# Top-k attention and GELU MLP: two of the four top-k rounds on a joined row, and a new order of ScalarE's steps

## The chip, the cores and the metric

The kernel runs on one core of a Trainium2 chip. A time is device microseconds of one execution. Beside the timed runs, one execution was taken by the hardware profiler; its rows are what is quoted below. The engines are PE (TensorE: matmuls; PEld is its weight load), DVE (VectorE), ACT (ScalarE), POOL (GpSimd) and SP (SyncE, here the DMA queue).

## The reference

Attention over 8 batches, 8 heads, 576 positions and 64 dimensions, in which each row keeps its 32 largest scores; then an MLP with exact GELU on the 4608 tokens.

```python
scores = scale * np.matmul(q, k.transpose(0, 1, 3, 2))            # 8 x 8 x 576 x 576
kth = np.partition(scores, -32, axis=-1)[..., -32:-31]
scores = np.where(scores >= kth, scores, -1e9)
attn = np.exp(scores - scores.max(-1, keepdims=True))
attn = attn / (attn.sum(-1, keepdims=True) + 1e-9)
x = np.matmul(attn, v)                                            # to (4608, 512)
h = x @ w_in                                                      # (4608, 2048)
out = (0.5 * h * (1 + erf(h / sqrt(2)))) @ w_out                  # (4608, 512)
```

## The kernel before, in words

**Items.** The work on attention is cut into 144 items, 18 for each batch. An item is a block of 128 query rows for two heads (e = 0, 1), so its scores are a tile `s` of 128 partitions by 2 x 576 values. The last 64 rows of each batch are put together from two pairs of heads. Where two batches meet, one has these items at its end and the next at its start.

**The order is written out by hand.** A loop over steps n = 0 to 147 issues, for several items at different stages, the instructions of each engine in the order in which that engine runs them; each engine works strictly through its own list and waits on semaphores. In step n:

- PE makes the scores of item n + 2 (`scores`, L370, and the last keys at L333 or L347), the product with v of item n - 3 (`attend`, L629), and the transposes of item n - 2 (`transposes`, L539 for the last keys and L565 for the others). Pieces of the MLP stand between these: L687 is the first layer into `h_ps`, L829 and L831 the second. Up to START (n = 10) there is no MLP work to put there, and `keep_busy` (L1015) issues a fixed number of filler matmuls instead.
- ACT copies the scores out of PSUM (L341, L378), runs the softmax of item n - 1 (`softmax`), copies the transposes (`pt`, L549, L572, L581), the attention output (`xT`, L634) and q and k (`qm`, `kt`, L286), and makes the GELUs (L703).
- DVE finds the 32nd largest score of item n in each row (`top_k`), with the reciprocal of item n - 1's sum put in near the end (`inverse`, L495).
- POOL makes the smaller list of item n + 1 (`smaller`, L431), adds 1e-9 to the sum of item n - 1 (`add_small`, `den`, L501), makes `neg` and `bias` of item n out of `kth` (`threshold`, L488, L489), multiplies item n - 1 by its reciprocal (`normalise`, L520), begins the lists of item n + 2 (`sum_up`, L423), and then takes small additions of the MLP (L724 to L727, L852 and L881 to L896).

**Top-k on pairs.** In 134 items (all but items 18 to 27, `SINGLE`) the 576 values of a row are split into two halves of 288, a and b. DVE makes the larger of each pair (`larger`, L406), POOL the smaller as a + b - larger in integer arithmetic. The two lists lie behind each other in a tile `lists` of 128 x 2 lists x 2 heads x 288. MAX8 (L463) finds the 8 largest of a list, MATCH_REPLACE8 (L466) overwrites them, and that is a round, for both heads. Before, the larger list has four rounds (32 values, the last without replacing) and the smaller list two (16 values, the second without replacing). The 17th to 32nd of the larger list and the 16 of the smaller one in reverse are then compared pairwise (L478), and the least of the results (L479) is `kth`, in a tile of its own. For items 0 and 1 the rest of the larger list goes to a tile `rest_g`. In the ten items that are not paired the same rounds run four times over all 576 values, and `kth` is the last value of `top`. `top` has one buffer.

**Softmax.** For each head, L508 applies a steep Prelu that throws out all that is below `kth`, in place, and L509 reads the result and makes the exponential and its sum. In steps up to START both heads follow each other with little between (the copy of `xT` in some steps).

**Weights.** For each of steps 1 to 10 and 13 to 18, at the end of the step before, a block of the MLP's weights is widened from its loaded form (`weights_size`): L205 and L206 on ACT, where L206 reads what L205 wrote, then L212, which works on another part and needs neither. In some of the later steps L208 on DVE takes the place of L212. POOL adds the two results (L227).

Of the kernel before, what the change touches and what calls it, by code (L numbers as in the profile page):

```python
# [8 lines left out]
TOPK = 32  # L9
LOWEST = -3.4028234e38  # L10
STEEP = 2.0**100
# [3 lines left out]
def kernel(  # L15
# [42 lines left out]
    scale = 1.0 / float(D) ** 0.5  # L58
# [4 lines left out]
    work = ctx.enter_context(tc.tile_pool(name="work", bufs=2))  # L63
# [90 lines left out]
    low = const.tile([P, 1], f32, name="low")  # L154
# [39 lines left out]
    def parts(u):  # L194

        t, dst = words[u], weights_of(u)[3].bitcast(i32)
        return t[:, :, 0::2], t.bitcast(mybir.dt.int16)[:, :, 2::4], t[:, :, 1::2], dst

    def weights_size(u):


        if u not in words:
            return
        w, first, below, d = parts(u)
        nc.scalar.activation(below, first, func=AF.Prelu, bias=high, scale=2.0**-40, alpha=2.0**40)  # L205
        nc.scalar.activation(d, below, func=AF.Prelu, bias=low, scale=2.0**59, alpha=2.0**-40)  # L206
        if on_dve(u):
            nc.vector.tensor_scalar(  # L208
                w.bitcast(i32), w.bitcast(u32), 2.0**-13, None, op0=ALU.mult
            )  # L210
        else:
            nc.scalar.activation(w.bitcast(i32), w.bitcast(u32), func=AF.Copy, scale=2.0**-13)  # L212

    def on_dve(u):

        return SLOT_OF[u] in ON_DVE

    def waits(u):

        return u == ORDER[-1]  # L220
# [25 lines left out]
    N = len(items)  # L246
# [60 lines left out]
    S_of, stat_of = {}, {}  # L307

    def row(i, e):
        return S_of[i][:, e * S : (e + 1) * S]  # L310
# [81 lines left out]
    lists_of = {}  # L392
    HS = S // 2

    def paired(i):

        return PAIRED <= i < N and i not in SINGLE

    def halves_of(i):
        s = S_of[i].rearrange("p (e h n) -> p e h n", e=2, h=2)  # L400
        return s[:, :, 0], s[:, :, 1]

    def larger(i):

        if paired(i):
            nc.vector.tensor_tensor(lists_of[i][:, 0], *halves_of(i), op=ALU.max)  # L406

    def first_lists():

        lists_of[0] = t = work.tile([P, 2, 2, HS], f32, tag="lists", name="lists")  # L410
        a, b = halves_of(0)
        for e in range(2):
            nc.vector.tensor_tensor(t[:, 0, e], a[:, e], b[:, e], op=ALU.max)
        top, both = t[:, 0].bitcast(i32), t[:, 1].bitcast(i32)
        nc.gpsimd.tensor_tensor(both, a.bitcast(i32), top, op=ALU.subtract)
        nc.gpsimd.tensor_tensor(both, both, b.bitcast(i32), op=ALU.add)

    def sum_up(i):

        if paired(i):  # L420
            lists_of[i] = t = work.tile([P, 2, 2, HS], f32, tag="lists", name="lists")
            a, b = halves_of(i)
            nc.gpsimd.tensor_tensor(  # L423
                t[:, 1].bitcast(i32), a.bitcast(i32), b.bitcast(i32), op=ALU.add
            )

    def smaller(i):

        if paired(i):
            both, top = lists_of[i][:, 1].bitcast(i32), lists_of[i][:, 0].bitcast(i32)  # L430
            nc.gpsimd.tensor_tensor(both, both, top, op=ALU.subtract)  # L431

    def top_k(i, last):


        stat_of[i] = st = {
            "first": work.tile([P, 2, 8], f32, tag="first", name="first"),
            "kth": work.tile([P, 2], f32, tag="kth", name="kth"),
            "neg": work.tile([P, 2], f32, tag="neg", name="neg"),
            "bias": work.tile([P, 2], f32, tag="bias", name="bias"),  # L440
            "den": work.tile([P, 2], f32, tag="den", name="den"),
            "rden": work.tile([P, 2], f32, tag="rden", name="rden"),
        }
        half_k = TOPK // 2
        top = work.tile([P, 2, TOPK - 8], f32, tag="top", bufs=1, name="top")
        low = work.tile([P, 2, half_k], f32, tag="low", bufs=1, name="low")
        into = [st["first"]] + [top[:, :, 8 * r : 8 * r + 8] for r in range(TOPK // 8 - 1)]
        if paired(i):
            t = lists_of.pop(i)
            rest = t[:, 0]  # L450
            if i < 2:
                rest = work.tile([P, 2, 512], f32, tag="g", bufs=2, name="rest_g")[:, :, 0:HS]
            rounds = [(t[:, 0] if r == 0 else rest, rest, x) for r, x in enumerate(into)]
            rounds += [(t[:, 1], t[:, 1], low[:, :, 8 * r : 8 * r + 8]) for r in range(half_k // 8)]
            ends = (len(into) - 1, len(rounds) - 1)
        else:
            s = S_of[i].rearrange("p (e n) -> p e n", e=2)
            t = work.tile([P, 2, S], f32, tag="lists", name="rest")
            rounds = [(s if r == 0 else t, t, x) for r, x in enumerate(into)]
            ends = (len(rounds) - 1,)  # L460
        for r, (src, dst, x) in enumerate(rounds):
            for e in range(2):
                nc.vector.max(x[:, e], src[:, e])  # L463
            if r not in ends:
                for e in range(2):
                    nc.vector.match_replace(dst[:, e], x[:, e], src[:, e], LOWEST)  # L466
# [7 lines left out]
        backwards = bass.AP(  # L474
            tensor=low.tensor, offset=low.offset + half_k - 1,
            ap=[list(low.ap[0]), [half_k, 2], [-1, half_k]],
        )
        nc.vector.tensor_tensor(upper, upper, backwards, op=ALU.max)  # L478
        nc.vector.tensor_reduce(  # L479
            st["kth"].rearrange("p (e x) -> p e x", x=1), upper, mybir.AxisListType.X, ALU.min  # L480
        )

    def threshold(i):

# [12 lines left out]
    def add_small(i):  # L497
# [2 lines left out]
        st = stat_of[i]  # L500
        nc.gpsimd.tensor_scalar(st["den"], st["den"], 1e-9, None, op0=ALU.add)  # L501

    def softmax(i, e):

        if i < 0 or i >= N:
            return
        st, s = stat_of[i], row(i, e)
        nc.scalar.activation(s, s, func=AF.Prelu, bias=st["neg"][:, e : e + 1], scale=1.0, alpha=STEEP)  # L508
        nc.scalar.activation(  # L509
            s, s, func=AF.Exp, bias=st["bias"][:, e : e + 1], scale=1.0,  # L510
            accum_out=st["den"][:, e : e + 1],
        )
# [84 lines left out]
    def copy_x():  # L597
        while copies:
            copies.pop()()
# [445 lines left out]
    for pair in range(2, n_pairs):  # L1045
        b, p = divmod(pair, NP)
# [9 lines left out]
    for n in range(ahead):  # L1056
# [7 lines left out]
        if n > 0:  # L1064
            larger(n + 1)
# [29 lines left out]
        if not few[0] and n > START:  # L1095
            softmax(n - 1, 0)
# [33 lines left out]
        if n > 0:  # L1130
            smaller(n + 1)
# [74 lines left out]
```

## Time and profile before

| | before |
|---|---|
| median of 3 runs | 1535.11 us (1534.01 to 1535.32) |
| the profiled execution's own time | 1534.11 us |
| its span, from the first to the last instruction | 1532.3 us |
| mean granted clock of TensorE | 0.998 |
| HBM read and written | 45.08 MB, 9.44 MB |

A row of the list of groups reads: line, engine, operation, output <- inputs, shapes, number of instructions, then busy time, mean duration in ns of one, and idle time of the engine just before it with what ended most of it. A row of the order of time reads: start in us from the span's start, duration in us, engine, line, operation, output <- inputs, shape, number merged into the row, and in brackets the idle time before it and what ended that. A row of a stretch of time reads: the stretch and its length, then for PE, PEld, DVE, ACT and POOL the busy time and the number of instructions, the granted clock, the busy share of the DMA engines and GB/s. A row of the waits reads: who waited for whom, us in total, how many times, and the longest.

### The profile page before, as it was taken

The page shows a single profiled execution, that of the slowest core. Times are in us where ns is not written, and L with a number is a line of the kernel's source. Part 1 is how long each engine was busy: PE and PEld are TensorE (multiplying, and loading weights), DVE is VectorE, ACT ScalarE, POOL GpSimd, SP SyncE. Part 2 cuts the span into 40 slices and gives each one's busy share as a digit, 9 for nine tenths or more (in the row PEclk, how much of TensorE's full clock was granted, in tenths as well). Part 3 has the DMA queues.
Part 4 walks back from the last instruction along what each step waited for, and adds up shares of the span by engine and source line. Part 5 has one row for each costly group of instructions (what it writes and reads, how often), then busy time and mean ns, then how long its engine had stood idle before and what let it go on. Part 6 is the DMA issues. An engine that isn't in the chain of part 4 may idle for free.

```text
span 1532.3 us, 28123 instructions
## 1 busy us (share of the span) xinstructions
PE 1513.8 (99%) x9240; PEld 1194.1 (78%) x9240; DVE 1336.5 (87%) x4610; ACT 1160.1 (76%) x2038; POOL 1144.5 (75%) x1291
## 2 busy tenths in 40 slices
PE   7999999999999999999999999999999999999999
PEld 5786677887777777888877778788787777788887
DVE  7999999999989988899989998989998998888801
ACT  6999977777877687877777777787777868787730
POOL 6897667767787878777787877776788786877742
PEclk9999999999999999999999999999999999999999
DMA  6434310012101110012201111012110111000000
GB/s 169 135 108 114 87 46 1 21 35 37 24 19 28 38 40 15 1 30 47 40 15 20 27 32 46 1 25 36 32 24 22 24 30 32 15 1 15 8 14 14
DMA packets 195026, 56.35 MB, mean 37 GB/s; under 512 B 185888, under 2 KB 186432, under 8 KB 194880
## 3 DMA queue, kind: packets, MB, share of 16 engines
q1 hardware_dynamic: 193616, 54.14, 15.2%
q8 instruction: 72, 1.18, 0.3%
q14 instruction: 74, 0.61, 0.1%
q10 hardware_dynamic: 1200, 0.39, 0.1%
q0 software_dynamic: 64, 0.03, 0.0%
HBM read 45.08 MB, written 9.44 MB: 36 GB/s over the span
## 4 chain that ended last, share of the span: by engine, by line
PE 75%; POOL 11%; DVE 5%; ACT 1%; issue 1%; DVEq 0%; POOLq 0%
PE h_ps L687 27%; PE y_ps L831 15%; PE o L629 8%; PE tp L565 6%; PE s_ps L370 6%; POOL s L520 3%; PE seven L829 2%; PE y_ps L775 2%; PE y_ps L793 2%; PE y_ps L796 2%; POOL lists L423 1%; POOL lists L431 1%; DVE lists L466 1%; PE tp_t L333 1%; PE o L640 1%; DVE top L463 1%
## 5 line engine op out<-in xcount | busy, mean ns | idle before, releaser
L687 PE MATMUL h_ps<-xT,w_in_sb 128*128 128x256 f32 (+1 forms) x2560 | 544.2, 361 | 0.2
L687 PEld LDWEIGHTS h_ps<-xT,w_in_sb 128*128 128x128 f32 x2560 | 434.0, 191 | 71.1 <-issue 25.2
L463 DVE MAX8 top<-lists 128x8 f32<-128x288 f32 x792 | 321.3, 447 | 0.0
L520 POOL TENSOR_TENSOR s<-s,rden 128x1152 f32<-128x1152 f32 x144 | 302.7, 2102 | 0.3 <-DVE rden L495 0.3
L509 ACT ACTIVATE s<-s,bias 128x576 f32<-128x576 f32 x288 | 223.4, 776 | 11.9
L466 DVE MATCH_REPLACE8 lists<-top,lists 128x288 f32<-128x288 f32 x528 | 229.9, 443 | 0.0
L508 ACT ACTIVATE s<-s,neg 128x576 f32<-128x576 f32 x288 | 225.7, 784 | 4.0 <-POOL neg L488 3.9
L581 ACT COPY pt<-tp 128x1024 f32<-128x1024 f32 x133 | 135.2, 1017 | 112.1 <-PE tp L565 112.1
L463 DVE MAX8 low<-lists 128x8 f32<-128x288 f32 x536 | 216.4, 446 | 0.0
L431 POOL TENSOR_TENSOR lists<-lists 128x576 int32<-128x576 int32 x133 | 187.6, 1410 | 4.0
L501 POOL TENSOR_SCALAR den<-den 128x2 f32<-128x2 f32 x144 | 31.4, 218 | 213.0 <-ACT s L509 208.8
L423 POOL TENSOR_TENSOR lists<-s 128x576 int32<-128x576 int32 x133 | 187.0, 1406 | 0.0
L488 POOL TENSOR_SCALAR neg<-kth 128x2 f32<-128x2 f32 x134 | 86.9, 649 | 99.2 <-DVE kth L479 98.1
L629 PEld LDWEIGHTS o<-pt,raw_v 128*64 128x64 f32 x1280 | 87.3, 137 | 86.5 <-issue 45.4
L629 PE MATMUL o<-pt,raw_v 128*64 128x256 f32 x1280 | 153.8, 385 | 0.7 <-ACT pt L572 0.4
L565 PE MATMUL tp<-ident,s 128*128 128x128 f32 x1152 | 149.6, 273 | 0.0
L565 PEld LDWEIGHTS tp<-ident,s 128*128 128x128 f32 x1152 | 134.7, 141 | 14.7 <-issue 1.9
L831 PE MATMUL y_ps<-w_out_sb,sum 128*128 128x256 f32 x472 | 140.4, 379 | 0.0
L370 PE MATMUL s_ps<-kt,qm 64*128 64x512 f32 x512 | 131.1, 626 | 0.8 <-ACT s L376 0.8
L378 ACT ACTIVATE s<-s_ps 128x1024 f32<-128x1024 f32 x127 | 124.0, 1024 | 8.9 <-PE s_ps L370 8.8
L495 DVE RECIPROCAL rden<-den 128x2 f32<-128x2 f32 x144 | 23.2, 161 | 115.3 <-POOL den L501 114.1
L466 DVE MATCH_REPLACE8 lists<-low,lists 128x288 f32<-128x288 f32 x268 | 116.7, 443 | 0.0
(164 smaller groups left out, 2770.9 us busy)
## 6 DMA issues: line engine op xcount, KB each, us to landing
raw_v<-in_v_dram SPq DMA_DIRECT2D x64, 128.0 KB, 2.4
out_dram<-y SPq DMA_DIRECT2D x30, 256.0 KB, 2.1
raw_q<-in_q_dram SPq DMA_DIRECT2D x112, 64.0 KB, 2.0
raw_k<-in_k_dram SPq DMA_DIRECT2D x112, 64.0 KB, 2.0
w_out_sb<-in_moe_w_in_dram SPq DMA_DIRECT2D x14, 511.8 KB, 4.7
w_out_sb<-in_moe_w_out_dram SPq DMA_DIRECT2D x10, 511.8 KB, 4.3
w_sum<-in_moe_w_out_dram SPq DMA_DIRECT2D x6, 511.8 KB, 4.7
raw_q<-in_q_dram SPq DMA_DIRECT2D x112, 8.0 KB, 1.8
```

The source lines that it names most:

```text
L370: nc.tensor.matmul(s_ps[:, e], lhsT=q_t[rows, :], rhs=kt[rows, 0:SM], start=True, stop=True)
L423: nc.gpsimd.tensor_tensor(t[:, 1].bitcast(i32), a.bitcast(i32), b.bitcast(i32), op=ALU.add)
L431: nc.gpsimd.tensor_tensor(both, both, top, op=ALU.subtract)
L463: nc.vector.max(x[:, e], src[:, e])
L466: nc.vector.match_replace(dst[:, e], x[:, e], src[:, e], LOWEST)
L508: nc.scalar.activation(s, s, func=AF.Prelu, bias=st["neg"][:, e : e + 1], scale=1.0, alpha=STEEP)
L509: nc.scalar.activation(s, s, func=AF.Exp, bias=st["bias"][:, e : e + 1], scale=1.0, accum_out=st["den"][:, e : e + 1],)
L520: nc.gpsimd.tensor_tensor(s, s, wide, op=ALU.mult)
L565: nc.tensor.transpose(tp[:, j * P : (j + 1) * P], s[:, first + j * P : first + (j + 1) * P], ident)
L629: nc.tensor.matmul(o[e * D : (e + 1) * D, 0:n], lhsT=vt[:, j, e, :], rhs=pt[:, e * NM + j if j < NM else 2 * NM, :], start=(j == 0), stop= ...
L687: nc.tensor.matmul(h_tile(u)[:, i, :], lhsT=w_in_sb[:, ko, f * P : (f + 1) * P], rhs=xT[:, ko, c0 : c0 + n], start=(ko == 0), stop=(ko == ...
L831: nc.tensor.matmul(acc[names][:, k], lhsT=lhsT, rhs=rhs, start=(j == 0 and k == 0), stop=(j == FT // 2 - 1 and k == 1),)
```

## The change

- In paired items the two lists now lie side by side for each head (128 x 2 heads x 2 lists x 288), so that both together are one row of 576 values. Two rounds run on the larger list, with replacing; then two rounds run on the joined row, which holds what is left of the larger list and the smaller list, the last without replacing. The pairwise comparison and the minimum are gone, and `kth` is the last value of `top` in all items.
- For items 0 and 1 the joined row is a tile `into`, which uses the buffer of `pt`, in place of `rest_g`.
- The instruction that follows L205 in `weights_size` is now the one on the other part, and the one that reads L205's result comes third.
- In steps up to START the Prelus of both heads are issued before the first exponential.

Line numbers of the changed file differ by a few: L463 becomes L465, L466 L468, L423 L431, L431 L439, L488 and L489 L479 and L480, L501 L492, L520 L522, L495 L486, L508 L499, L509 L511, L539 L541, L687 L689.

```diff
         nc.scalar.activation(below, first, func=AF.Prelu, bias=high, scale=2.0**-40, alpha=2.0**40)
-        nc.scalar.activation(d, below, func=AF.Prelu, bias=low, scale=2.0**59, alpha=2.0**-40)
         if on_dve(u):
...
             nc.scalar.activation(w.bitcast(i32), w.bitcast(u32), func=AF.Copy, scale=2.0**-13)
+        nc.scalar.activation(d, below, func=AF.Prelu, bias=low, scale=2.0**59, alpha=2.0**-40)
...
     def larger(i):
         if paired(i):
-            nc.vector.tensor_tensor(lists_of[i][:, 0], *halves_of(i), op=ALU.max)
+            nc.vector.tensor_tensor(lists_of[i][:, :, 0], *halves_of(i), op=ALU.max)
+
+    def into_of(i):
+        if i < 2 and i not in into_lists:
+            into_lists[i] = work.tile([P, 2, 2, HS], f32, tag="pt", bufs=1, name="into")
+        return into_lists.get(i, lists_of[i])
...
     def sum_up(i):
...
-                t[:, 1].bitcast(i32), a.bitcast(i32), b.bitcast(i32), op=ALU.add
+                t[:, :, 1].bitcast(i32), a.bitcast(i32), b.bitcast(i32), op=ALU.add
...
     def smaller(i):
         if paired(i):
-            both, top = lists_of[i][:, 1].bitcast(i32), lists_of[i][:, 0].bitcast(i32)
-            nc.gpsimd.tensor_tensor(both, both, top, op=ALU.subtract)
+            both, top = lists_of[i][:, :, 1].bitcast(i32), lists_of[i][:, :, 0].bitcast(i32)
+            nc.gpsimd.tensor_tensor(into_of(i)[:, :, 1].bitcast(i32), both, top, op=ALU.subtract)
...
     def top_k(i, last):
...
         if paired(i):
-            t = lists_of.pop(i)
-            rest = t[:, 0]
-            if i < 2:
-                rest = work.tile([P, 2, 512], f32, tag="g", bufs=2, name="rest_g")[:, :, 0:HS]
-            rounds = [(t[:, 0] if r == 0 else rest, rest, x) for r, x in enumerate(into)]
-            rounds += [(t[:, 1], t[:, 1], low[:, :, 8 * r : 8 * r + 8]) for r in range(half_k // 8)]
-            ends = (len(into) - 1, len(rounds) - 1)
+            t = lists_of[i]
+            u = into_of(i)
+            both = u.rearrange("p e h n -> p e (h n)")
+            rounds = [(t[:, :, 0], u[:, :, 0]), (u[:, :, 0], u[:, :, 0])]
+            rounds = [(*(rounds[r] if 16 * r < TOPK else (both, both)), x) for r, x in enumerate(into)]
...
-        if not paired(i):
-            st["kth"] = top[:, :, TOPK - 9]
-            return
-        upper = top[:, :, half_k - 8 :]
...
-        nc.vector.tensor_tensor(upper, upper, backwards, op=ALU.max)
-        nc.vector.tensor_reduce(
-            st["kth"].rearrange("p (e x) -> p e x", x=1), upper, mybir.AxisListType.X, ALU.min
-        )
+        st["kth"] = top[:, :, TOPK - 9]
...
-    def softmax(i, e):
+    def select(i, e):
...
         nc.scalar.activation(s, s, func=AF.Prelu, bias=st["neg"][:, e : e + 1], scale=1.0, alpha=STEEP)
+        selected.add((i, e))
+
+    def softmax(i, e):
...
+        if (i, e) not in selected:
+            select(i, e)
...
         if n < START:
+            for e in range(2):
+                select(n - 1, e)
             softmax(n - 1, 0)
         copy_x()
         if n == START:
+            for e in range(2):
+                select(n - 1, e)
             softmax(n - 1, 0)
```

More of the change, by code (lines that the diff above doesn't have):

```diff
@@ L405, in larger @@
         if paired(i):
-            nc.vector.tensor_tensor(lists_of[i][:, 0], *halves_of(i), op=ALU.max)
+            nc.vector.tensor_tensor(lists_of[i][:, :, 0], *halves_of(i), op=ALU.max)
[3 more added lines that the diff above has]
+        return into_lists.get(i, lists_of[i])
+    into_lists = {}
     def first_lists():
@@ L412, in first_lists @@
         for e in range(2):
-            nc.vector.tensor_tensor(t[:, 0, e], a[:, e], b[:, e], op=ALU.max)
-        top, both = t[:, 0].bitcast(i32), t[:, 1].bitcast(i32)
+            nc.vector.tensor_tensor(t[:, e, 0], a[:, e], b[:, e], op=ALU.max)
+        top, both = t[:, :, 0].bitcast(i32), into_of(0)[:, :, 1].bitcast(i32)
         nc.gpsimd.tensor_tensor(both, a.bitcast(i32), top, op=ALU.subtract)
@@ L437, in top_k @@
             "first": work.tile([P, 2, 8], f32, tag="first", name="first"),
-            "kth": work.tile([P, 2], f32, tag="kth", name="kth"),
             "neg": work.tile([P, 2], f32, tag="neg", name="neg"),
@@ L459, in top_k @@
             rounds = [(s if r == 0 else t, t, x) for r, x in enumerate(into)]
-            ends = (len(rounds) - 1,)
         for r, (src, dst, x) in enumerate(rounds):
@@ L463, in top_k @@
                 nc.vector.max(x[:, e], src[:, e])
-            if r not in ends:
+            if r < len(rounds) - 1:
                 for e in range(2):
@@ L501, in add_small @@
         nc.gpsimd.tensor_scalar(st["den"], st["den"], 1e-9, None, op0=ALU.add)
+    def select(i, e):
+        if i < 0 or i >= N:
+            return
+        st, s = stat_of[i], row(i, e)
+        nc.scalar.activation(s, s, func=AF.Prelu, bias=st["neg"][:, e : e + 1], scale=1.0, alpha=STEEP)
+        selected.add((i, e))
+    selected = set()
     def softmax(i, e):
@@ L507, in softmax @@
         st, s = stat_of[i], row(i, e)
-        nc.scalar.activation(s, s, func=AF.Prelu, bias=st["neg"][:, e : e + 1], scale=1.0, alpha=STEEP)
+        if (i, e) not in selected:
+            select(i, e)
         nc.scalar.activation(
```

6 lines of the change are left out of this document (removed).

## The prediction

> **What bounds the kernel now.** I read the span and busy shares first, then the busy time in stretches of 50 us, then every place where TensorE (PE) sat idle, then the other engines' order of time around those places.
>
> ```profile
> span 1532.3 us, 28123 instructions
> PE 1513.8 (99%) x9240; PEld 1194.1 (78%) x9240; DVE 1336.5 (87%) x4610; ACT 1160.1 (76%) x2038; POOL 1144.5 (75%) x1291
> ```
>
> ```profile
> 0.00:50.00 50.00, 37.99 (x226) 28.48 (x226) 41.86 (x150) 36.73 (x59) 34.37 (x40) 0.94 0.65 177
> 700.00:750.00 50.00, 50.00 (x284) 38.77 (x282) 47.95 (x168) 39.70 (x68) 36.92 (x42) 1.00 0.22 41
> ```
>
> PE is idle for 18.5 us in all (1532.3 - 1513.8), and 12.0 of these lie in the first 50 us. A stretch from the middle shows PE at 50.00 of 50.00 us at full clock while DVE has 2 us to spare: DVE is the second busiest engine, not the bound. So the question is not what DVE saves, but which of PE's few idle places go. In order of time, the largest that anything in the change can reach:
>
> ```profile
> 36.50 0.44 PE L281 MATMUL tp_qk<-ident,w_sum 128*128 128x128 f32 x2 [1.59 <-ACT pt L549]
> 47.55 0.58 PE L333 MATMUL t_ps<-kt,qm 128*128 128x128 f32 x2 [2.66 <-ACT qm L286]
> ...
> 104.76 0.33 PE L539 MATMUL tp_t<-ident,s 128*128 128x128 f32 x1 [0.28 <-POOL s L520]
> 104.92 1.03 PE L687 MATMUL h_ps<-xT,w_in_sb 128*128 128x256 f32 x4
> ...
> 106.23 1.39 PE L687 MATMUL h_ps<-xT,w_in_sb 128*128 128x256 f32 x4
> ```
>
> ```profile
> PE tp_t L539 <- POOL s L520: 1.6, 7, 0.3
> DVE rden L495 <- POOL den L501: 114.1, 86, 8.1
> ```
>
> Before 50 us PE waits for ACT; between 50 us and the end its only repeated wait is that of L539 for POOL's normalising multiply, 7 times. Most of what DVE has to spare (114.1 us) it spends waiting for `den`, and ACT and POOL make that.
>
> **DVE's rounds.** Each of the 134 paired items loses two rounds on 288 values and the merge, and has two of its rounds on 576 values instead. The trace has both kinds, the wide one in the items not paired:
>
> ```profile
> 12.63 0.81 DVE L463 MAX8 top<-rest_g 128x8 f32<-128x288 f32 x2
> 13.36 0.07 DVE L466 MATCH_VALUE_LOAD rest_g<-top,rest_g 128x8 f32 x1
> ...
> 14.21 0.81 DVE L463 MAX8 top<-rest_g 128x8 f32<-128x288 f32 x2
> ...
> 18.08 0.81 DVE L463 MAX8 low<-lists 128x8 f32<-128x288 f32 x2
> ...
> 19.25 1.42 DVE L406 TENSOR_TENSOR lists<-s 128x576 f32<-128x576 f32 x2
> ```
>
> ```profile
> 196.13 1.41 DVE L463 MAX8 top<-rest 128x8 f32<-128x576 f32 x2
> 197.46 0.07 DVE L466 MATCH_VALUE_LOAD rest<-top,rest 128x8 f32 x1
> ...
> 198.90 1.41 DVE L463 MAX8 top<-rest 128x8 f32<-128x576 f32 x2
> ```
>
> A full narrow round takes 14.21 - 12.63 = 1.58 us, a full wide one 198.90 - 196.13 = 2.77. Before: four full narrow rounds, two pairs of MAX8 alone (13.36 - 12.63 = 0.73 each) and the merge (19.25 - 18.08 less 0.73 = 0.44): 8.22 us. After: 2 x 1.58 + 2.77 + a wide pair alone (197.46 - 196.13 = 1.33) = 7.26. That is 0.95 us an item, some 125 us of DVE's busy time. On the end I count it at nothing: PE has no idle time in those steps, and PE's list of instructions is unchanged. Were DVE the bound, it would be 8%; the 114.1 us row says that DVE would only wait longer.
>
> **ACT in the first steps.** The two other edits act in the steps up to START (n = 10), and there ACT sets the pace: the two gaps of 1.59 and 2.66 us end with an ACT copy, while no ACT row of these steps shows a wait. Part of the step ahead of the gap of 1.59 us:
>
> ```profile
> 28.46 1.25 ACT L205 ACTIVATE w_out_sb<-w_out_sb,high 128x1024 f32<-128x1024 int16 x1
> 29.74 1.25 ACT L206 ACTIVATE w_in_sb<-w_out_sb,low 128x1024 int32<-128x1024 f32 x1
> 30.88 1.17 ACT L212 ACTIVATE w_out_sb<-w_out_sb 128x1024 int32<-128x1024 uint32 x1
> ...
> 32.97 0.79 ACT L508 ACTIVATE s<-s,neg 128x576 f32<-128x576 f32 x1
> 33.86 0.78 ACT L509 ACTIVATE s<-s,bias 128x576 f32<-128x576 f32 x1
> 34.54 0.19 ACT L509 ACTIVATION_READ_ACCUMULATOR s<-s,bias 128x1 f32 x1
> 34.63 0.76 ACT L508 ACTIVATE s<-s,neg 128x576 f32<-128x576 f32 x1
> 35.42 0.78 ACT L509 ACTIVATE s<-s,bias 128x576 f32<-128x576 f32 x1
> ```
>
> L206 reads what L205 wrote and starts 0.03 us after its end; L212 reads nothing of L206 and starts 0.11 before its end. So a dependence costs 0.14 us, and with L212's work put between, it goes. In the softmax, L509 starts 0.10 after the end of the first L508 (33.76) and 0.03 after that of the second (35.39), where the accumulator read starts 0.10 before the end of what it follows: 0.20 and 0.13, together 0.33, of which I take 0.30. Three such steps (n = 1 to 3) and three weight units lie before the gap that ends at 47.55: 3 x (0.14 + 0.30) = **1.3 us** by which PE restarts sooner. Since nothing that ACT needs in these steps comes late, I let its chain move as a whole.
>
> From 47.55 to 104.48 PE runs its own fixed list with filler matmuls and has no gap; the savings of steps 4 to 10 only let ACT catch up with it. They are worth something once: at 104.76 PE waited for POOL (0.28 idle, and about 0.16 for a pipeline that ran empty; the seams below show that surplus), and I put it down to the same lateness that the h matmuls at 106.23 took 1.39 us where those at 104.92 took 1.03. Six steps of 0.44 us bring ACT's results, and so POOL's, 2.6 us earlier, over and above the 1.3 us by which PE comes earlier itself: both places go, **0.8 us**.
>
> The Trainium skill, ScalarE: Activation LUTs, section What ACT_TABLE_LOAD costs, says that back-to-back ACTIVATEs overlap by about 93 ns and makes no difference for dependent ones; by it this reordering would bring nothing. The rows agree for the independent pair (0.11) and differ for the dependent ones, and the rows decide.
>
> **The seams between batches.** The other six waits of L539 are one case, the first of them at 509.44:
>
> ```profile
> 508.72 0.45 PE L347 MATMUL tp_t<-kt 128*64 128x64 f32 x8
> 509.44 0.33 PE L539 MATMUL tp_t<-ident,s 128*128 128x128 f32 x1 [0.27 <-POOL s L520]
> ...
> 529.79 0.45 PE L347 MATMUL tp_t<-kt 128*64 128x64 f32 x8
> 530.17 0.33 PE L539 MATMUL tp_t<-ident,s 128*128 128x128 f32 x1
> ```
>
> ```profile
> 504.21 1.41 POOL L431 TENSOR_TENSOR lists<-lists 128x576 int32<-128x576 int32 x1
> 505.70 0.22 POOL L501 TENSOR_SCALAR den<-den 128x2 f32<-128x2 f32 x1
> 506.51 0.66 POOL L488 TENSOR_SCALAR neg<-kth 128x2 f32<-128x2 f32 x1 [0.59 <-DVE kth L479]
> 507.14 0.19 POOL L489 TENSOR_TENSOR bias<-kth,first 128x2 f32<-128x2 f32 x1
> 507.29 2.10 POOL L520 TENSOR_TENSOR s<-s,rden 128x1152 f32<-128x1152 f32 x1
> ```
>
> Without the wait L539 starts 0.38 us after L347 (530.17 - 529.79), here 0.72: a seam costs 0.34. POOL goes from L431 straight to `den` (504.21 + 1.41 = 505.62), then it stands 0.59 us, because `kth` comes behind `rden` and the merge on DVE. After the change `kth` is the last MAX8, ahead of `rden`, so L488 can follow `den` at once. One of L488 and L489 may be held longer than now, since DVE's L406 then starts beside them, so of the 0.59 I count 0.4, with bounds 0.1 (0.66 against 0.19, were L489 held like L488) and 0.59. The step ahead has the same wait, which makes 0.8 against 0.34 late. The six go: 6 x 0.34 = **2.0 us**; by the lower bound (0.2 in two steps) 6 x 0.14 = 0.8 of it stays.
>
> **New waits.** `kth` is now a view of `top`, which has one buffer: the next item's second MAX8 pair waits until L488 and L489 have read it. All of DVE's queue stands behind it. Between `den` and this pair lie `rden`, L406 (half of 1.42) and a narrow round (1.58), at least 2.3 us, and L489 ends 507.33 - 505.70 = 1.6 us after `den` even as things are, so the pair waits for nothing. ACT's first `pt` copy, the one that ends the gap at 36.50, now waits for the second item's top-k, which ends near 19.25 + 1.42 + 7.26 = 27.9. The smaller values are read from the third round on instead of the fifth; POOL made them a step ahead. No DMA or queue is moved.
>
> **Sum.** 1.3 + 0.8 + 2.0 = 4.1 us from the profiled execution (1534.11, span 1532.3): 1530.0. That execution lies 1.0 below the median of the runs shown (1535.11), and against the median it is **1531.0 us**, a gain of 0.27%.
>
> **The rivals.**
> *The clock comes too.* Two stretches run at half clock (the column of 0.50), right behind the gaps of 1.59 and 2.66 us:
>
> ```profile
> 37.60:41.00 3.40, 3.40 (x12) 1.90 (x11) 3.40 (x12) 3.37 (x5) 3.17 (x4) 0.50 1.03 330
> 47.90:51.10 3.20, 3.20 (x12) 1.15 (x12) 3.20 (x13) 3.17 (x5) 3.20 (x3) 0.50 0.00 0
> ```
>
> The first is hidden by the gap behind it; the second costs 3.2 x 0.5 = 1.6 us. If the shortened gap leaves the clock alone: 1529.4. Against it: PE reaches that gap two steps' saving (0.9) sooner and leaves it three steps' (1.3) sooner, so it shrinks by 0.4 of 2.66 only.
> The Trainium skill, TensorE: Matmul & The Clock Gate, section What's actually happening, puts the half rate behind at least one idle window of about 3.4 us, free-running. By it gaps below 3 us would often cost no clock, and the loss would change from run to run; the trace, with gaps of 1.59 and 2.66, shows it costs clock sooner.
>
> *Only ACT's part counts.* If POOL's queue, not `kth`, keeps the seams late, 2.1 us remain: 1533.0. For it speaks that POOL is full there; against it the 0.59 us.
>
> *It does nothing* that can be told from no change: the restart at 47.55 is lost again, PE being the bound: 1534.5.
>
> *Slower: POOL's lists.* L423 and L431 now write and read 288-value pieces with gaps:
>
> ```profile
> L431 POOL TENSOR_TENSOR lists<-lists 128x576 int32<-128x576 int32 x133 | 187.6, 1410 | 4.0
> L423 POOL TENSOR_TENSOR lists<-s 128x576 int32<-128x576 int32 x133 | 187.0, 1406 | 0.0
> ```
>
> L423 already reads two inputs with such gaps and takes what the flat L431 takes, so I price it at 0; bounds -0.05 and +0.5 an instruction. With d more in each, four of them (two a step) lie in the two steps of a seam's chain: up to d = 0.2 the freed 0.8 pays; above, six seams lose 4d - 0.8 each more than now. At d = 0.45 that is 6 us less the 2.1 of ACT's part: 1539.0; the time passes that of before from d = 0.29.
>
> **How the numbers follow.** Forecast 0.58, clock too 0.12, only ACT 0.17, nothing 0.08, slower 0.05. What a measurement of this kernel can tell from no change is about 0.2%, 3.1 us: faster means below 1532.0, slower above 1538.2. The forecast's own range is 1530.2 to 1532.5: 0.8 us of the seams staying on the one side, and half of the 1.3 us by which the three runs shown differ on both, so about a tenth of its chance falls within 0.2%. Faster 0.53 + 0.12 = 0.65; within 0.05 + 0.17 + 0.08 = 0.30; slower 0.05. The range for 8 in 10 reaches from the clock's case to that of ACT alone, each with those 0.65 us: 1528.7 to 1533.7.
>
> **What would show it.** In the changed profile: DVE's busy share falls by about 125 us and its wait for `den` grows by as much; PE's gap at 47.55 ends near 46.2; dependent ACT pairs are no longer seen before 105 us; L539 has no wait for POOL left; L488 follows L501 without 0.59 us; L423 and L431 stay at 1.41. It is wrong if PE's busy time changes by more than 2 us, if a gap opens between 47 and 104 us, or if POOL's list work grows.

## The result, and the profile after

| | before | after |
|---|---|---|
| median of 6 runs each, on the same chip | 1535.20 us (1534.01 to 1535.49) | 1529.09 us (1527.94 to 1530.76) |
| after / before | | 0.9962, 95% interval 0.9949 to 0.9975 |
| profiled execution, time and span | 1534.11, 1532.3 us | 1529.69, 1527.2 us |
| mean granted clock | 0.998 | 0.998 |

The kernel is 0.38% faster: 6.1 us between the medians, 4.4 between the two profiled executions and 5.1 between their spans. The forecast was 1531.0 in a range of 1528.7 to 1533.7, so the sign and the range held, and the forecast lay 1.9 us above the measured median. The interval of the ratio, 3.8 to 7.8 us of gain, is wider than that miss. The sections below say which terms were off.

From the page of after, the span, the busy time of the engines, and how the chain of work that ended last divides among the engines, with the same line of before behind it:

```profile
span 1527.2 us, 26934 instructions
PE 1509.6 (99%) x9240; PEld 1192.7 (78%) x9240; DVE 1235.7 (81%) x3270; ACT 1156.4 (76%) x2038; POOL 1150.5 (75%) x1291
PE 96%; ACT 1%; DVE 0%; issue 0%; DVEq 0%
```

```profile
PE 75%; POOL 11%; DVE 5%; ACT 1%; issue 1%; DVEq 0%; POOLq 0%
```

DVE lost 100.8 us of work (1336.5 - 1235.7) and 1340 instructions. PE has 9240 instructions in both. Before, 11% of the chain were on POOL; now it is PE nearly throughout.

Two stretches of time of after, in the columns of those shown of before (PE, PEld, DVE, ACT, POOL, clock):

```profile
0.00:50.00 50.00, 36.66 (x232) 27.41 (x234) 40.57 (x116) 37.29 (x61) 36.42 (x41) 0.95 0.64 177
700.00:750.00 50.00, 50.00 (x283) 38.68 (x282) 44.19 (x121) 38.82 (x67) 37.16 (x41) 1.00 0.21 40
```

In the first 50 us PE stood idle for 13.3 us (50.00 - 36.66), 1.3 more than before. In the middle of the run DVE went from 47.95 to 44.19 of 50 us and PE stayed at 50.00: nothing came of that there. After's waits of DVE for `den`:

```profile
DVE rden L486 <- POOL den L492: 216.8, 134, 8.5
```

From 114.1 to 216.8 us: +102.7, against 100.8 of work that went. All of DVE's saving became waiting.

**Where time is won, by items.** PE's list is the same in all kernels here but for filler matmuls, so the start of the first transpose of each of the 144 items (L539 or L565 before, L541 or L567 after) tells where time is won. Against before (its starts in the head of the table), in us:

| kernel | 53.92 | 104.76 | 123.33 | 1464.27 | won between the last two |
|---|---|---|---|---|---|
| after | -0.32 | -1.02 | -1.54 | -5.02 | 3.48 |

So 1.54 us come from the first 123 us, and 3.48 from ten places behind: 299.25, 509.44, 592.94, 602.32, 872.37, 955.87, 965.24, 1235.29, 1318.80 and 1328.18 us, each 0.23 to 0.40. (The first lies where the items that are not paired end, the others lie around three seams.) Between them the two kernels run in step.

### The profile page after: what moved, and what is told of

Same layout as the page of the kernel before. It is cut to its first block, busy times and chain, and to the rows that moved or that the text cites. A ratio compares the mean times of both kernels' runs of the same rounds, so it can differ in the third digit from the quotient of the medians.

```text
span 1527.2 us, 26934 instructions
## 1 busy us (share of the span) xinstructions
PE 1509.6 (99%) x9240; PEld 1192.7 (78%) x9240; DVE 1235.7 (81%) x3270; ACT 1156.4 (76%) x2038; POOL 1150.5 (75%) x1291
## 4 chain that ended last, share of the span: by engine, by line
PE 96%; ACT 1%; DVE 0%; issue 0%; DVEq 0%
PE h_ps L689 34%; PE y_ps L833 20%; PE o L631 10%; PE tp L567 8%; PE s_ps L370 8%; PE seven L831 3%; PE warm L1017 2%; PE y_ps L795 2%; PE y_ps L777 2%; PE y_ps L798 2%; PE tp_t L333 2%; PE o L642 1%; PE s_ps L385 1%; PE tp_t L541 1%; PE tp_t L347 0%; PE tp_t L544 0%
## 5 line engine op out<-in xcount | busy, mean ns | idle before, releaser
L689 PE MATMUL h_ps<-xT,w_in_sb 128*128 128x256 f32 (+1 forms) x2560 | 544.1, 362 | 0.0
L689 PEld LDWEIGHTS h_ps<-xT,w_in_sb 128*128 128x128 f32 x2560 | 434.1, 191 | 70.6 <-issue 25.2
L465 DVE MAX8 top<-lists 128x8 f32<-128x576 f32 (+1 forms) x792 | 476.7, 640 | 0.1
L468 DVE MATCH_REPLACE8 lists<-top,lists 128x288 f32<-128x288 f32 (+1 forms) x528 | 307.1, 586 | 0.0
L522 POOL TENSOR_TENSOR s<-s,rden 128x1152 f32<-128x1152 f32 x144 | 304.8, 2116 | 0.3 <-DVE rden L486 0.3
L492 POOL TENSOR_SCALAR den<-den 128x2 f32<-128x2 f32 x144 | 31.4, 218 | 282.8 <-ACT s L511 280.8
L511 ACT ACTIVATE s<-s,bias 128x576 f32<-128x576 f32 x288 | 223.5, 777 | 10.7
L499 ACT ACTIVATE s<-s,neg 128x576 f32<-128x576 f32 x288 | 224.8, 786 | 0.0
L486 DVE RECIPROCAL rden<-den 128x2 f32<-128x2 f32 x144 | 23.7, 165 | 217.1 <-POOL den L492 216.8
L439 POOL TENSOR_TENSOR lists<-lists 128x576 int32<-128x576 int32 x132 | 186.3, 1412 | 4.0
L431 POOL TENSOR_TENSOR lists<-s 128x576 int32<-128x576 int32 x133 | 187.0, 1406 | 0.0
L567 PE MATMUL tp<-ident,s 128*128 128x128 f32 x1152 | 149.7, 273 | 0.0
L567 PEld LDWEIGHTS tp<-ident,s 128*128 128x128 f32 x1152 | 134.6, 141 | 14.7 <-issue 1.9
L468 DVE MATCH_REPLACE8 lists<-first,lists 128x288 f32<-128x288 f32 x264 | 114.0, 436 | 0.0
L833 PE MATMUL y_ps<-w_out_sb,g 128*128 128x256 f32 x480 | 113.4, 379 | 0.0
L705 ACT ACTIVATE g<-h_ps 128x512 f32<-128x512 f32 x144 | 78.2, 595 | 42.1 <-PE h_ps L689 41.4
```

The lines of the kernel that those rows point to most:

```text
L431: nc.gpsimd.tensor_tensor(t[:, :, 1].bitcast(i32), a.bitcast(i32), b.bitcast(i32), op=ALU.add)
L439: nc.gpsimd.tensor_tensor(into_of(i)[:, :, 1].bitcast(i32), both, top, op=ALU.subtract)
L511: nc.scalar.activation(s, s, func=AF.Exp, bias=st["bias"][:, e : e + 1], scale=1.0, accum_out=st["den"][:, e : e + 1],)
L522: nc.gpsimd.tensor_tensor(s, s, wide, op=ALU.mult)
L567: nc.tensor.transpose(tp[:, j * P : (j + 1) * P], s[:, first + j * P : first + (j + 1) * P], ident)
L689: nc.tensor.matmul(h_tile(u)[:, i, :], lhsT=w_in_sb[:, ko, f * P : (f + 1) * P], rhs=xT[:, ko, c0 : c0 + n], start=(ko == 0), stop=(ko == ...
```

## The experiments

Three accounts stood after the result. **A**, the prediction's: the seams are mended because `kth` is there ahead of `rden`, and ACT's order wins its own part at the start. **B**: the seams are mended because DVE's rounds are shorter, wherever `kth` stands. **C**: the top-k part brings everything, and what ACT's order wins is lost again to the clock.

**x1_topk_only and x2_act_only: each part of the change alone.** x1 is after with ACT's two orders as before; x2 is before with ACT's two new orders. Of x1's edit:

```diff
 x1 (against after)
+        nc.scalar.activation(d, below, func=AF.Prelu, bias=low, scale=2.0**59, alpha=2.0**-40)
         if on_dve(u):
...
-        nc.scalar.activation(d, below, func=AF.Prelu, bias=low, scale=2.0**59, alpha=2.0**-40)
...
-            for e in range(2):
-                select(n - 1, e)
             softmax(n - 1, 0)
```

> The new top-k alone, with ACT's order of before. Theory A (the seams go because kth no longer stands behind rden on DVE; the head of the kernel is ACT's alone): PE restarts near 47.55 us as before, the late places at 104 to 118 us stay, and the ten delays of L541 at the batch seams (3.5 us in all) go: about 3.5 us below before, 1531.7. Rival C (the head's gain also comes from DVE's shorter rounds): PE restarts near 46.0 and the time is about 1529 to 1530.

> ACT's two new orders alone, with the old top-k. Theory A: PE restarts near 46.0 us, the seams keep their 3.5 us, 1.5 us below before: 1533.7. Rival C: less than half of the 1.5 us, 1534.7 or more. If ACT's new order also mended the seams, 1530 to 1531.

x1: 1530.60 us (1530.38 to 1531.63, 6 runs) against 1535.51, ratio 0.9971 (0.9959 to 0.9982). x2: 1532.71 (1531.99 to 1533.70, 11 runs) against the same, 0.9985 (0.9976 to 0.9994). Both parts make the kernel faster, so C falls, and so does a rival in which one part does it all. Both came out about 1 us below A's figures. The items' starts divide the gain cleanly:

| kernel | 53.92 | 104.76 | 123.33 | 1464.27 | won between the last two |
|---|---|---|---|---|---|
| x1_topk_only | -0.11 | -0.50 | -0.37 | -3.85 | 3.48 |
| x2_act_only | -0.25 | -0.95 | -1.44 | -1.52 | 0.08 |
| x3_kth_first | +0.36 | +0.07 | +0.13 | -3.35 | 3.48 |
| x4_kth_late | -1.40 | -2.10 | -2.52 | -3.38 | 0.86 |

The seams are the top-k's alone, to the hundredth (3.48 against 0.08); nearly all of the first 123 us is ACT's.

**x3_kth_first and x4_kth_late: the place of `kth`, apart from the length of the rounds.** x3 is before, rounds and merge as they were, with the reciprocal put behind the merge; x4 is after with two small instructions like the merge (a maximum of the last 16 values of `top` with themselves, and a minimum) put behind the reciprocal, so that `kth` again ends late:

```diff
 x3 (against before)
-            if r == len(rounds) - 1:
+            if r == len(rounds) - 1 and not paired(i):
                 last()
...
             st["kth"].rearrange("p (e x) -> p e x", x=1), upper, mybir.AxisListType.X, ALU.min
         )
+        last()
```

```diff
 x4 (against after)
-        st["kth"] = top[:, :, TOPK - 9]
+        if not paired(i):
+            st["kth"] = top[:, :, TOPK - 9]
+            return
+        st["kth"] = work.tile([P, 2], f32, tag="kth", name="kth")
+        upper = top[:, :, 8:]
+        nc.vector.tensor_tensor(upper, upper, upper, op=ALU.max)
+        nc.vector.tensor_reduce(
+            st["kth"].rearrange("p (e x) -> p e x", x=1), upper, mybir.AxisListType.X, ALU.min
+        )
```

> The kernel of before with one thing changed: in paired items the merge (L478) and kth (L479) stand ahead of the reciprocal on DVE instead of behind it; DVE has as much work as before. Theory A: L488 follows L501 at once, L539 at the seams waits no more, 3.5 us below before: 1531.7. Rival B (the seams go because DVE has 0.95 us less to do in an item): nothing is gained, 1535.2, or it is slower by some tenths, since rden comes 0.4 us later where DVE is late.

> The changed kernel with the two small instructions of the old merge put back behind the reciprocal (they yield the same kth), so that kth is late again while DVE's rounds stay short. Theory A: the 0.59 us between L501 and the next POOL instruction are back and most of the 3.5 us at the seams with them: 1532 to 1533. Rival B: the seams stay mended, 1529.1 to 1529.5.

x3: 1531.48 us (1530.36 to 1532.72, 8 runs), ratio 0.9974 (0.9964 to 0.9985): a move of two instructions, with no work saved, brings all 3.48 us of the seams. POOL around the seam at 509.44, first in after, then in x3:

```profile
503.02 0.22 POOL L492 TENSOR_SCALAR den<-den 128x2 f32<-128x2 f32 x1
503.32 0.22 POOL L479 TENSOR_SCALAR neg<-top 128x2 f32<-128x2 f32 x1
503.50 0.67 POOL L480 TENSOR_TENSOR bias<-top,first 128x2 f32<-128x2 f32 x1
504.13 2.10 POOL L522 TENSOR_TENSOR s<-s,rden 128x1152 f32<-128x1152 f32 x1
```

```profile
504.68 0.22 POOL L502 TENSOR_SCALAR den<-den 128x2 f32<-128x2 f32 x1
504.98 0.22 POOL L489 TENSOR_SCALAR neg<-kth 128x2 f32<-128x2 f32 x1
505.15 0.67 POOL L490 TENSOR_TENSOR bias<-kth,first 128x2 f32<-128x2 f32 x1
505.79 2.10 POOL L521 TENSOR_TENSOR s<-s,rden 128x1152 f32<-128x1152 f32 x1
```

In both, `neg` follows `den` by 0.30 us, where it stood 0.59 idle before, and from `den` to the multiply are 1.11 us instead of 1.59. DVE has no less to do in x3: it is busy for 1379.6 us, before for 1336.5. The seams are mended all the same.

x4: 1530.66 us (1530.50 to 1531.82, 7 runs), 0.9971 (0.9960 to 0.9982). A's figure was missed by over 1.3 us and B's by 1.2, and the median alone decides little here, since x4 won 2.52 us at the start, where after, with the same instructions for ACT, won 1.54 (see below on the clock). By the items' starts behind 123 us it can be decided: 0.86 of the 3.48 stay. They come from three places, 509.44, 872.37 and 1235.29, and not because the wait for `kth` went there: it is 0.59 us as before (503.64 in x4). They come from two steps earlier, where DVE itself was late in before. POOL of before, then of x4:

```profile
485.14 0.66 POOL L488 TENSOR_SCALAR neg<-kth 128x2 f32<-128x2 f32 x1 [1.01 <-DVE kth L479]
```

```profile
482.21 0.66 POOL L487 TENSOR_SCALAR neg<-kth 128x2 f32<-128x2 f32 x1 [0.59 <-DVE kth L478]
```

The 0.42 us less reach the seam, since POOL's queue is full from there on. At the other seven places POOL and PE wait as before, for instance, POOL and then PE of x4:

```profile
596.58 0.66 POOL L487 TENSOR_SCALAR neg<-kth 128x2 f32<-128x2 f32 x1 [0.59 <-DVE kth L478]
```

```profile
599.51 0.33 PE L549 MATMUL tp_t<-ident,s 128*128 128x128 f32 x1 [0.19 <-POOL s L530]
```

So A holds, and B for 0.86 of 3.48 us: shorter rounds do it where DVE's own work was late, and the place of `kth` does it everywhere.

**x5_gaps_filled: the clock at the start.** In after PE still stands idle before 50 us and then runs at half clock. **D**: that costs 2 to 2.8 us, which comes and goes with the run; filler matmuls in the gaps keep the clock. **E**: nothing is to be had there, since ACT or POOL set the pace at once. The edit puts 24 more filler matmuls (each two instructions in the trace) where PE is idle:

```diff
 x5 (against after)
+        if n == 2:
+            keep_busy(4, ident)
...
-            keep_busy(8, ident)
+            keep_busy(14, ident)
+        if n == 3:
+            keep_busy(14, ident)
```

> The changed kernel with more filler matmuls in the three places before 50 us where PE waits for ACT (6 more calls in step 1, 4 in step 2, 14 at the end of step 3; a call is about 0.23 us of PE), so that PE is hardly idle there. Theory D (the half clock behind the gap of 3.83 us costs 2.8 us of PE: scores 2.08 against 1.13 us, the product with v 3.92 against 2.38; and it is what makes the runs of one kernel differ by up to 2.8 us): no stretch at half clock after 10 us, PE reaches 120 us some 2 to 2.8 us sooner, 1526.5 to 1527, and the runs lie closer together. Rival E (ACT or POOL take over as the pace at once): 1529.

x5: 1526.78 us (1526.43 to 1527.05, 5 runs) against 1535.14, ratio 0.9946 (0.9933 to 0.9958). D's gain is there. PE of after around the gap, the whole stretch of time at half clock, then the same rows of PE of x5 and a stretch of time behind the gap:

```profile
46.02 0.80 PE L333 MATMUL t_ps<-kt,qm 128*128 128x128 f32 x2 [3.83 <-ACT qm L286]
46.74 2.08 PE L370 MATMUL s_ps<-kt,qm 64*128 64x512 f32 x4
48.75 3.92 PE L631 MATMUL o<-pt,raw_v 128*64 128x256 f32 x20
```

```profile
45.10:51.90 6.80, 5.88 (x22) 2.83 (x24) 6.80 (x20) 6.80 (x10) 6.52 (x5) 0.50 0.00 1
```

```profile
46.62 0.49 PE L333 MATMUL t_ps<-kt,qm 128*128 128x128 f32 x2 [0.71 <-ACT qm L286]
47.03 1.13 PE L370 MATMUL s_ps<-kt,qm 64*128 64x512 f32 x4
48.09 2.38 PE L631 MATMUL o<-pt,raw_v 128*64 128x256 f32 x20
```

```profile
47.00:51.00 4.00, 4.00 (x30) 2.25 (x30) 4.00 (x13) 4.00 (x6) 3.67 (x3) 1.00 0.00 0
```

The filler makes PE start 0.6 us later (46.62 against 46.02) and PE is still further on two rows later: the three rows take 3.9 us from the first start to the last end instead of 6.7.

Two signs of D are less clear. It said that no stretch at half clock would be left after 10 us; one is there, from 18.8 to 22.2 us, at the end of a wait of 2.83 us for a transfer, into which the edit puts no filler. And the runs of x5 lie within 0.6 us, those of after within 2.8; but those of x6, with the same filler in the gaps, lie within 1.5, and those of x4, without it, within 1.3. That the spread is the clock's is therefore not shown.

**x6_less_filler and x7_before_filled: what sets the pace next.** With the clock held from 22 us on, steps 5 to 10 of x5 run at the length of their own filler (**F**). x6 takes 2 of the 28 filler matmuls away in the steps among these that have so many. x7 puts filler into before's gaps; if ACT sets before's pace there, it should win little, and it tells how much of x5 is the clock alone:

```diff
 x6 (against x5)
-            keep_busy((4 if product or n == 0 else 14) * (1 if n < 5 else 2), ident)
+            keep_busy((4 if product or n == 0 else 14 if n < 5 else 13) * (1 if n < 5 else 2), ident)
```

```diff
 x7 (against before)
+        if n == 2:
+            keep_busy(6, ident)
...
-            keep_busy(8, ident)
+            keep_busy(16, ident)
+        if n == 3:
+            keep_busy(10, ident)
```

> The kernel of x5_gaps_filled with 26 in place of 28 filler calls in every second step from step 5 on. Theory F (with ACT's new order PE's filler sets the pace of steps 5 to 10): up to 0.47 us less in each of three pairs of steps, 1.0 to 1.4 us below x5_gaps_filled. Rival E (ACT sets it as soon as the half clock is gone): as x5_gaps_filled, with waits of PE for POOL or ACT near 104 us.

> The kernel of before with more filler in the same three places (8, 6 and 10 calls). Theory D with ACT as the pace of steps 5 to 10: the half clock goes here too, but PE then only waits longer for ACT and POOL at 104 to 118 us, so 0.3 to 1.2 us below before, 1534.0 to 1534.9. Rival (the clock alone is the pace): 1.6 us or more below before.

x6: 1525.62 us (1525.53 to 1527.03, 5 runs), ratio to before 0.9941 (0.9927 to 0.9955); x7: 1534.37 (1533.59 to 1535.14, 11 runs), 0.9995 (0.9987 to 1.0004), so no difference from before that can be told.

| kernel | 53.92 | 104.76 | 123.33 | 1464.27 | won between the last two |
|---|---|---|---|---|---|
| x5_gaps_filled | -2.52 | -3.22 | -3.69 | -7.14 | 3.45 |
| x6_less_filler | -3.00 | -4.77 | -5.16 | -8.64 | 3.48 |
| x7_before_filled | +0.31 | +0.33 | +0.33 | +0.28 | 0.05 |

One of the three blocks of filler that the edit shortens, in x5 and then in x6:

```profile
72.80 6.52 PE L1017 MATMUL warm<-ident 128*128 128x128 f32 x56
```

```profile
72.14 6.07 PE L1017 MATMUL warm<-ident 128*128 128x128 f32 x52
```

Three times 0.45 us is 1.35, and x6 wins 1.07 (4.77 - 3.22 is 1.55, less the 0.48 that it is ahead at 53.92) in these steps: F holds. The 0.28 that is missing went at one place: the product with v that starts at 62.88 in x6 took 2.65 us, and 2.38 in x5 (at 63.80). Between 50 and 100 us ACT's busy time rose from 49.43 us in x5 to 50.00 in x6. ACT is now full as well, so still less filler should only make PE wait for it, which was not tried. x7 shows the other side. Its rows at the same gap:

```profile
47.81 0.49 PE L333 MATMUL t_ps<-kt,qm 128*128 128x128 f32 x2 [2.07 <-ACT qm L286]
48.23 1.71 PE L370 MATMUL s_ps<-kt,qm 64*128 64x512 f32 x4
```

x7's time is in the range expected, but only one of the two stretches at half clock went: a gap of 2.07 us was left here, and half clock behind it (the scores take 1.71 us, at full clock 1.13); so x7 is no full test of before without the clock's loss, only of this much filler. x6 is the fastest kernel of this study: 9.5 us below the median of the runs of before that were taken with it.

## Why the prediction was right, and which sizes were off

By the items' starts, of the 5.02 us 3.48 come from the seams (forecast 2.0) and 1.54 from the first 123 us (forecast 1.3 + 0.8 = 2.1). The second sum has a step in it that failed: of the 1.3 us for the earlier restart only 0.32 were left at 53.92, while the places at 104 to 118 us brought 1.22 instead of 0.8. So it was in part luck that the total came close: +1.5 at the seams and +0.4 at 104 to 118 us stand against -1.0 at the restart.

One of the prediction's own signs of being wrong also appeared. It named a change of PE's busy time by more than 2 us, and that fell by 4.2 (1513.8 - 1509.6), while PE's idle time fell by only 0.9 (18.5 to 17.6). The prediction looked for the gain in PE's idle time. But in this profile a matmul at half clock counts as busy, and so does most of a late start under the modelled end of the matmul ahead of it (see the next paragraph): 4.2 of the 5.1 us by which the span got shorter were never idle time in it.

**The seams: right in the mechanism, 1.5 us too small.** That `kth` ahead of `rden` frees POOL, and not the shorter rounds, is what x3 and x4 show. Of the 0.59 us of idle I counted 0.4 as won, and from `den` to the multiply it is 0.48; the hold that I feared moved from `neg` to `bias` (0.67 us at 503.50). What the sum missed is how many places there are. I took the six waits of PE that the view of waits names; ten places won time. At the other four L539 started late with next to no idle time in front of it in PE's row, since PE's ends are modelled and the end modelled for L333 (592.85 below) left only 0.09 us. PE of before at one of them, then of after:

```profile
592.47 0.38 PE L333 MATMUL tp_t<-kt,qm 128*128 128x128 f32 x2
592.94 0.33 PE L539 MATMUL tp_t<-ident,s 128*128 128x128 f32 x1
```

```profile
590.30 0.38 PE L333 MATMUL tp_t<-kt,qm 128*128 128x128 f32 x2
590.52 0.27 PE L541 MATMUL tp_t<-ident,s 128*128 128x128 f32 x1
```

From start to start 0.47 us became 0.22: 0.25 us at a place with no bracket in either row. Four such make 1.0, the six visible ones came to 2.2 against 2.0, and 0.05 to 0.06 more was won one item behind each of four places.

The wait was not hidden everywhere, though. The prediction quoted the row of PE (1.6 us, 7 times); the same view of before has one of PEld, the weight load of the same matmul, and so has the order of time:

```profile
PEld tp_t L539 <- POOL s L520: 4.8, 13, 0.7
```

```profile
592.94 0.14 PEld L539 LDWEIGHTS tp_t<-ident,s 128*128 128x128 f32 x1 [0.28 <-POOL s L520]
```

All ten places are among the 13, with 0.26 to 0.42 us each. They come to 3.4 us, and 3.48 were won. Two of the other three are 104.76 and 113.88 (0.73 and 0.43). In after this row is gone.

**ACT's order: right up to the restart.** PE restarts at 46.02 instead of 47.55, 1.53 us sooner, where 1.3 was forecast; most of that was lost again (see the clock). The three instructions of a weight block and the first two of a softmax, ACT of after:

```profile
19.88 1.26 ACT L205 ACTIVATE w_out_sb<-w_out_sb,high 128x1024 f32<-128x1024 int16 x1
21.03 1.18 ACT L211 ACTIVATE w_out_sb<-w_out_sb 128x1024 int32<-128x1024 uint32 x1
22.09 1.23 ACT L212 ACTIVATE w_in_sb<-w_out_sb,low 128x1024 int32<-128x1024 f32 x1
23.22 0.26 ACT L341 ACTIVATE s<-t_ps 128x128 f32<-128x128 f32 x1
24.28 1.44 ACT L499 ACTIVATE s<-s,neg 128x576 f32<-128x576 f32 x2
25.61 0.77 ACT L511 ACTIVATE s<-s,bias 128x576 f32<-128x576 f32 x1
```

Within a group, each starts 0.10 to 0.12 us before the end of the one ahead. The block of weights takes 3.44 us to the end of its last instruction (22.09 + 1.23 - 19.88), and 3.59 before (30.88 + 1.17 - 28.46): 0.15, with 0.14 forecast. For 104 to 118 us (late results of POOL and ACT at START) the forecast was 0.8: from 53.92 to 123.33 the lead grew by 1.54 - 0.32 = 1.22.

**The clock: this step failed.** "It shrinks by 0.4 of 2.66 only" is what the prediction says of the gap at 47.55. It grew, to 3.83 us, and the stretch at half clock behind it got longer: 6.8 us, from 45.1 to 51.9, where before had 3.4 (47.8 to 51.2). Scores and product took 5.9 us from 46.74 (48.75 + 3.92 - 46.74), before 4.9 (48.07 to 53.00). So of the 1.53 us won at the restart 0.32 were left at 53.92. The gap grew because of the stretch that I took as hidden. Part of PE's order of time in after, and then, in before, the same scores and the two rows behind the second gap:

```profile
35.41 0.43 PE L281 MATMUL tp_qk<-ident,w_sum 128*128 128x128 f32 x2 [1.10 <-ACT pt L551]
...
36.32 1.13 PE L370 MATMUL s_ps<-kt,qm 64*128 64x512 f32 x4
```

```profile
37.40 1.96 PE L370 MATMUL s_ps<-kt,qm 64*128 64x512 f32 x4
...
48.07 2.08 PE L370 MATMUL s_ps<-kt,qm 64*128 64x512 f32 x4
50.08 2.92 PE L629 MATMUL o<-pt,raw_v 128*64 128x256 f32 x20
```

With the first gap at 1.10 us instead of 1.59, the clock stayed: the scores took 1.13 us instead of 1.96, PE came to the second gap 2.7 us sooner (47.55 - 2.66 = 44.89 against 46.02 - 3.83 = 42.19) and so waited there longer. The rival in which the clock comes too was thus half right: one of the two stretches went, and that one won nothing, because it lay ahead of a gap that ACT ends. That the other stretch doubled doesn't follow from the longer gap alone: x4 has a gap as long (3.76 us) and behind it half clock for 3.4 us only, and keeps 1.40 us at 53.92 where after keeps 0.32. x5 shows the price of what stayed: 2.3 us between the medians.

The Trainium skill, TensorE: Matmul & The Clock Gate, section What's actually happening, says that the window in which activity is counted runs freely, so that the loss differs from run to run. The traces agree: after and x4, with the same order on ACT, stand 1.1 us apart at 53.92 (-0.32 and -1.40). They agree also with the window's length, some 3.4 us by the same section: every stretch at half clock that they record before 60 us is one or two times 3.41 us long. What they show otherwise is that a window needn't be idle throughout: half clock came behind gaps of 1.59, 2.07 and 2.66 us.

**DVE's rounds: worth nothing at all on the end, as said.** The saving was 0.75 us an item (100.8 / 134) rather than 0.95, a difference that no run here explains, and all of it turned into waiting. x3 shows it from the other side: with none of that saving, the seams' whole gain. x4 limits it: where `kth` stays late, the shorter rounds are worth 0.86 us.

**The priced-at-nothing terms.** DVE's wait for `top` before its second MAX8 pair, and POOL's list instructions on pieces with gaps, groups of after:

```profile
L431 POOL TENSOR_TENSOR lists<-s 128x576 int32<-128x576 int32 x133 | 187.0, 1406 | 0.0
L439 POOL TENSOR_TENSOR lists<-lists 128x576 int32<-128x576 int32 x132 | 186.3, 1412 | 4.0
L465 DVE MAX8 top<-lists 128x8 f32<-128x288 f32 x264 | 106.2, 441 | 0.1
```

1406 and 1412 ns against 1406 and 1410, and 0.1 us of idle before 264 instructions: the rival in which the kernel gets slower had no price.

**From the profiled execution to the median.** I added 1.0 us, as if the profiled execution of after would lie as far below its median as that of before. It lay 0.6 above. The medians differ by 6.1 = 4.4 + 1.1 (before's profiled execution below its median of 1535.20) + 0.6. The 21 runs of before that were taken with x1 to x4 have spans of 1532.5 to 1534.3, in two groups, near 1532.6 and 1533.9; the profiled one, 1532.3, is of the lower sort. Whether these groups are the clock's is open: the upper group has a granted clock of 0.997 throughout, the lower one 0.996 to 0.998. The gains of x1 and x2 between medians, 4.9 and 2.8 us, add up to more than 6.1, but their intervals are 2.8 to 6.3 and 0.9 to 3.7 us, and by the items' starts they are 3.85 + 1.52 = 5.37 against 5.02.

## What to carry to other kernels

In a pipeline where one engine is full, look at what stands between a small result and the engine that waits for it: moving two instructions ahead of a wait won 3.48 us here, and less work on an engine that was not the bound (DVE, 66 us less in x4 than before) won 0.86 of them by itself. Compare two traces by the start times of the same matmuls, item by item, and read the waits of the weight load beside those of the matmul, for a late start can hide under a modelled end where the matmul's own row shows no idle time. And where a fixed amount of filler keeps an engine warm, check after every change whether it still fills the gaps, and whether it has become the pace itself.

## What the runs showed of the hardware

**Half clock behind short gaps, in steps of 3.41 us.** PE fell to 0.50 behind idle gaps of 1.59 us (before, at 36.50), 2.07 (x7) and 2.66 (before, at 47.55), and stayed at full clock behind 1.10 (after) and 0.71 (x5). The length of a gap doesn't decide it alone. After and x4 wait for the same transfer, 2.50 and 2.48 us long, and only x4 loses the clock behind it. PE and then a stretch of time of after, and the same of x4:

```profile
18.73 0.63 PE L281 MATMUL tp_qk<-ident,raw_k 128*128 128x128 f32 x4 [2.50 <-DMA raw_k<-in_k_dram]
```

```profile
20.00:22.80 2.80, 2.80 (x24) 2.23 (x21) 2.80 (x10) 2.80 (x3) 2.10 (x2) 1.00 0.39 85
```

```profile
18.91 0.63 PE L281 MATMUL tp_qk<-ident,raw_k 128*128 128x128 f32 x4 [2.48 <-DMA raw_k<-in_k_dram]
```

```profile
20.00:22.80 2.80, 2.80 (x8) 1.30 (x9) 2.80 (x12) 2.80 (x4) 2.56 (x2) 0.50 0.50 110
```

The edges of the stretches at half clock lie on a grid of 3.41 us in each trace: in before at 37.57, 40.98, 47.81 and 51.23, in x4 at 19.45, 22.86, 46.75 and 50.16, in after at 45.10 and 51.92. An estimate: with the grid carried back from these edges, x4's gap (16.43 to 18.91) lies within one step of it (16.04 to 19.45), and after's (16.23 to 18.73) is split by a line at 17.80. That fits the two. It doesn't explain everything: a gap of 1.62 us, at 28.03 in after, lies within one step by the same estimate and left the clock alone, where 1.59 at 36.50 in before did not. The loss at 19.45 in x4 didn't reach the end: PE comes to 28.15 there without idle time, where after stands idle for 1.62 us until 28.03. The one behind the gap before 50 us did: by it after and x4 differ by 1.1 us at 53.92.

**A two-column instruction on POOL held by DVE.** `bias` works on 128 x 2 values and took 0.67 us at 503.50, as long as DVE's `larger` with its two inputs was at work beside it; before, it was `neg` that started beside it and took 0.66. DVE of after:

```profile
503.36 0.76 DVE L406 TENSOR_TENSOR lists<-s 128x576 f32<-128x576 f32 x1
```

L406 ends at 504.12 and `bias` at 504.17. Over all 144 items, groups of after:

```profile
L480 POOL TENSOR_TENSOR bias<-top,first 128x2 f32<-128x2 f32 x144 | 89.8, 624 | 0.0
L479 POOL TENSOR_SCALAR neg<-top 128x2 f32<-128x2 f32 x144 | 35.4, 246 | 18.7 <-DVE rden L486 4.8 <-DVE top L465 3.0
```

The Trainium skill, SBUF — State Buffer, section SBUF: two separate sides, says that DVE with two inputs from SBUF and POOL share a pair of ports that one holds for its whole instruction; the ends at 504.12 and 504.17 fit that.
